# Delta rule and gated layers on one core: the first four chunks solved by rows in two passes, and the whole order written anew

## The chip, the core and the metric

One core of one Trainium2 chip runs the program. TensorE (PE) multiplies, VectorE (DVE), ScalarE (ACT) and GpSimd (POOL) work elementwise, and SyncE (SP) issues most of the transfers. The metric is the device time of one execution in microseconds (us), lower is better.

## The reference

The program computes a delta-rule attention over 768 positions for 4 x 8 heads of width 48, and puts its output through two dense layers with a gate between them.

```python
k_n = k / (np.linalg.norm(k, axis=-1, keepdims=True) + 1e-06)
for t in range(S):                       # S = 768, state is 48 x 48 a head
    y[:, :, t] = np.einsum('bhd,bhde->bhe', q[:, :, t], state)
    v_old = np.einsum('bhde,bhd->bhe', state, kt)
    state = state + bt[:, :, :, None] * np.einsum('bhd,bhe->bhde', kt, vt - v_old)
...
h = x @ w_in                             # x is 3072 x 384, w_in 384 x 2048
g = h - np.tanh(h)
return (g @ w_out).astype(np.float32)    # w_out 2048 x 384
```

## The kernel before

**Chunks and groups.** The 768 positions are cut into 24 chunks of C = 32. In a chunk each of the 32 heads (4 batches x 8) has a 32 x 32 triangular system. Four chunks make a group, so a group has 128 systems, one in each partition, and is solved on DVE. There are six groups; `solve(g, k)` issues step k of group g.

**A group's solve.** PE forms the Gram products of the keys (`gram` for chunks 0 to 3, `pair` for the others, which also forms the query products). `gather` copies four chunks' Gram matrices into one tile, and step 0 transposes it in 32 x 32 blocks so that a partition holds one system. Some eighteen instructions on 32 elements normalize the keys, the square root by Newton steps (for group 0 by ScalarE's table). Then column j of the system is eliminated by two instructions, `times` (a product into the scratch tile `ta`) and `plus`, for j = 1 to 30. In groups 1 to 5 each of them is issued as two instructions over separate columns where 5 < j < 27 (`spans`). A last transposition writes `tt`, the solved triangles, in the layout that PE multiplies with.

**Group 0 is halved.** Its systems are cut into two 16 x 16 triangles that are solved in the same instructions (`JOINED`), j = 1 to 14 only; the missing quarter is put together afterwards for each chunk by two small PE products (`join_a`, `join_b`) with a copy on ScalarE between them (`join_y`) and an addition on DVE (`join_u`).

**Chunk by chunk.** The chunks follow each other through the 48 x 48 states: `keyed` (K, old state times keys and queries), `vsub` (vs), `chunk` (C, solved triangle times values), `spread` (sd, a copy), `answer` (A), the update (U, summed into the PSUM tile `sums`), `keep` (kp, the state copied to SBUF), then the output turned by PE (`turn`, tu) and split into a high and a low part (`x_high` xh, `x_low` xl).

**Dense layers.** Four chunks are a wave of 512 columns; there are six. A wave takes 16 steps f. `hidden` (h) makes 128 hidden features with 9 matmuls, `tanh` (th, ScalarE), `gate` (ga, DVE), `gate_high` and `gate_low` (gh, gl) split the gate's output, and `output` (o) adds 9 matmuls into the PSUM tile `po`. The first wave is done in two halves of 256 columns, z = 0 for chunks 0 and 1, z = 1 for chunks 2 and 3.

**Weights.** The 32 weight pieces of 384 KB are loaded in pairs and split on ScalarE and DVE into two f32r parts: `sign` (dr), `low_bits` (db), `merge` (dm), `high` (dh), `low` (dl). A pair costs ScalarE three and DVE two instructions of 768 elements.

**Order.** The string `ORDER` is the program: each item names an engine and an operation, and an engine executes its items in that order. A wait comes only from data and from buffers that are used again. A load is marked S1 to S4: it is not issued before the load that stands that many loads ahead of it has landed. SP executes its items in order too, so a load that waits for its buffer holds up all loads behind it. `fi:n` issues n matmuls whose result nobody uses.

Of the kernel before, what the change touches and what calls it, by code (L numbers as in the profile page):

```python
# [44 lines left out]
def kernel(ctx: ExitStack, tc: tile.TileContext, kp, kn, vn, beta, w_in, w_out, const, out):  # L45
# [38 lines left out]
    def open_():  # L84
        nc.vector.memset(wz, 0.0)
        nc.vector.memset(sums[32:64, :, :DM], 0.0)

    def const_():
        nc.scalar.dma_start(cs[:, :260], const)
        nc.scalar.activation(wz[:, 0:1], wz[:, 0:1], AF.Sqrt)  # L90
# [34 lines left out]
    def gram(s, slot):  # L125
        ps = hc(bank(slot, f"g{s}"))
        for u in range(16):
            products(s, ps[:, :, :C], live[f"k{s}"], 0, u)
# [37 lines left out]
    nm, ss, zz, sq, gm = small.values()  # L166
    solves = {}

    def solve(g, k, *slots):
        if g not in solves:  # L170
            solves[g] = steps(g)
        solves[g][k](*slots)

    def steps(g):
        halves = g in JOINED
        gs = live[f"gs{g}"]
        V = nc.vector
        ax = lambda: live[f"a{g}"]
        sq3 = lambda: ax()[:, :C * C].rearrange("p (i c) -> p i c", c=C)
        flat = lambda: ax()[:, :C * C]  # L180

        def turn(slot):
            make("sol", slot, f"a{g}", [128, 1056])
            V.transpose(flat(), gs[:, :C * C])

        do = [turn, lambda: V.tensor_copy(sq, flat()[:, ::C + 1])]
        do.append(lambda: V.tensor_scalar(ss, sq, 1e-30, None, ALU.max))
        if g == 0:
# [7 lines left out]
                lambda: V.scalar_tensor_tensor(gm, gm, 4.0, live["bt0"], ALU.mult, ALU.mult),  # L196
                lambda: V.tensor_scalar(nm, nm, 0.5, None, ALU.mult)]
        else:
            do.append(lambda: V.tensor_scalar(nm.bitcast(I32), ss.bitcast(I32), -0.5, 1597463007.0, ALU.mult, ALU.add))
            for _ in range(3):  # L200
                do += [
                    lambda: V.scalar_tensor_tensor(zz, ss, -0.5, nm, ALU.mult, ALU.mult),
                    lambda: V.tensor_tensor(zz, zz, nm, ALU.mult),
                    lambda: V.scalar_tensor_tensor(nm, zz, 1.5, nm, ALU.add, ALU.mult)]
            do += [
                lambda: V.tensor_tensor(nm, nm, sq, ALU.mult),
                lambda: V.tensor_scalar(nm, nm, 1e-6, None, ALU.add),
                lambda: V.tensor_tensor(gm, nm, nm, ALU.mult),
                lambda: V.reciprocal(gm, gm),
                lambda: V.tensor_tensor(gm, gm, live[f"bt{g}"], ALU.mult)]  # L210
        do.append(lambda slot: V.transpose(make("nt", slot, f"nt{g}", [128, C]), nm))
        size = C // 2 if halves else C
        nb = C // size

        def part():
            if halves:
                return ax().rearrange("p (x r) -> p x r", x=2)[:, :, :512].rearrange("p x (i c) -> p x i c", c=C)[:, :, :, :size]
            return sq3()

        P = lambda i, j: part()[:, :, i, j] if nb == 2 else part()[:, i, j]  # L220

        def scale(x):
            block = part()[:, x] if nb == 2 else part()
            V.scalar_tensor_tensor(block, block, -1.0, gm[:, size * x:size * x + size, None].broadcast_to([128, size, size]), ALU.mult, ALU.mult)

        do += [lambda x=x: scale(x) for x in range(nb)]
        do.append(lambda: nc.gpsimd.memset(flat()[:, ::C + 1], 1.0))

        def scratch(j):
            n = size - 1 - j  # L230
            tv = ta[:, j % 2 * 256:j % 2 * 256 + nb * n * j]
            if nb == 2:
                return tv.rearrange("p (x i c) -> p x i c", c=j, x=2), [128, 2, n, j]
            return tv.rearrange("p (i c) -> p i c", c=j), [128, n, j]

        def spans(j):
            if nb == 2 or not 5 < j < 27:
                return (slice(0, j),)
            x = 4 if j < 14 else 10
            return (slice(0, x), slice(x, j))  # L240

        def times(j):
            tv, dims = scratch(j)
            for x in spans(j):
                d = dims[:-1] + [x.stop - x.start]
                V.tensor_tensor(tv[..., x], P(slice(j + 1, size), slice(j, j + 1)).broadcast_to(d),  # L246
                                P(slice(j, j + 1), x).broadcast_to(d), ALU.mult)

        def plus(j):
            tv, _ = scratch(j)  # L250
            for x in spans(j):
                rest = P(slice(j + 1, size), x)
# [582 lines left out]
```

## Time and profile before

| | |
|---|---|
| median of 3 runs | 594.34 us (592.3 to 596.8) |
| span of the profiled execution, first to last instruction | 588.6 us |
| PE busy | 558.4 us, 95% |
| DVE busy | 379.7 us, 65% |
| ACT busy | 187.5 us, 32% |
| granted TensorE clock, mean | 0.985 of full speed |

The page gives the profiled execution's span alone; the median of the runs lies 5.7 us above it, the lowest run 3.7 us. The busy shares are means over a beginning in which PE has little to do and a long rest in which it has no pause, so the stretches are read one by one.

### The profile page before, as it was taken

Reading aid. Unit: us, or ns where it says so; the run is one execution under the profiler, and the core shown is the slowest. Engines: PE = TensorE matmul, PEld = TensorE weight load, DVE = VectorE, ACT = ScalarE, POOL = GpSimd, SP = SyncE. Lnnn points to the kernel's source line nnn. Section 1 sums busy time; section 2 is a strip of 40 time slices with the busy share of each in tenths; the row PEclk is TensorE's granted clock in tenths of the full one; section 3 lists DMA queues with packets and bytes.
Section 4 is the critical chain, followed back from the end, with each engine's and each line's share of the span. In section 5 each row is a group of like instructions: output and inputs, shape, how many; then the busy total and the mean of one; then the engine's idle time right before and its main releaser. Section 6 shows DMA issues by size and latency. Waiting matters only on the chain.

```text
span 588.6 us, 25934 instructions
## 1 busy us (share of the span) xinstructions
PE 558.4 (95%) x11943; PEld 458.4 (78%) x11943; DVE 379.7 (65%) x1089; ACT 187.5 (32%) x330; POOL 39.0 (7%) x44
## 2 busy tenths in 40 slices
PE   4848899999999999999999999999999999999997
PEld 3444788899998888788888788787888888888885
DVE  4899997899768995569965333599824322533242
ACT  1447776333313222232222223132320323322211
POOL 0000001100100000000000000200010000001111
PEclk9967999999999999999999999999999999999999
DMA  7778753331325100433312103221210100000001
GB/s 203 236 235 288 220 157 106 107 96 52 105 94 158 47 14 11 144 86 106 91 48 83 30 1 111 70 63 60 62 29 33 52 2 3 1 33 22 2 0 53
DMA packets 21517, 48.82 MB, mean 83 GB/s; under 512 B 3232, under 2 KB 9760, under 8 KB 21408
## 3 DMA queue, kind: packets, MB, share of 16 engines
q1 hardware_dynamic: 20864, 46.44, 26.0%
q8 instruction: 93, 1.52, 1.1%
q10 hardware_dynamic: 544, 0.72, 0.4%
q14 instruction: 16, 0.13, 0.1%
HBM read 42.44 MB, written 4.72 MB: 80 GB/s over the span
## 4 chain that ended last, share of the span: by engine, by line
PE 87%; DVE 9%; issue 2%; DMA 1%; ACT 1%
PE po L514 35%; PE ph L479 34%; PE sums L361 3%; PE g L123 3%; PE pu L351 3%; PE kk L340 3%; PE py L367 2%; PE py L355 2%; DVE ta L246 2%; DVE a L253 2%; PE px L412 1%; DVE raw L447 1%; DMA k<-in_kp 1%; DVE w L457 1%; DMA raw<-in_w_in 1%
## 5 line engine op out<-in xcount | busy, mean ns | idle before, releaser
L514 PE MATMUL po<-gh,w 128*128 128x512 f32 (+1 forms) x1008 | 221.6, 366 | 0.0
L479 PE MATMUL ph<-xt,w 128*128 128x512 f32 (+1 forms) x1008 | 218.4, 364 | 0.5 <-DVE t L492 0.4
L479 PEld LDWEIGHTS ph<-xt,w 128*128 128x128 f32 x1008 | 170.1, 189 | 31.6 <-DVE t L492 0.5
L514 PEld LDWEIGHTS po<-gh,w 128*128 128x128 f32 x1008 | 168.5, 189 | 30.3 <-DVE gh L502 0.2
L492 DVE TENSOR_TENSOR t<-ph,t 128x512 f32<-128x512 f32 (+1 forms) x112 | 68.2, 611 | 108.6 <-ACT t L487 108.4
L487 ACT ACTIVATE t<-ph 128x512 f32<-128x512 f32 (+1 forms) x112 | 59.7, 538 | 192.7 <-PE ph L479 144.7
L502 DVE TENSOR_TENSOR gh<-t,gh 128x512 fp32r<-128x512 f32 (+1 forms) x89 | 54.4, 614 | 26.0 <-ACT gh L497 25.3
L497 ACT CAST gh<-t 128x512 fp32r<-128x512 f32 (+1 forms) x63 | 35.8, 570 | 83.1 <-PE po L514 52.9
L253 DVE TENSOR_TENSOR a<-a,ta 128x108 f32<-128x108 f32 (+28 forms) x269 | 60.4, 257 | 1.5
L246 DVE TENSOR_TENSOR ta<-a 128x108 f32<-128x108 f32 (+28 forms) x269 | 59.6, 254 | 1.3
L502 POOL TENSOR_TENSOR gh<-t,gh 128x512 fp32r<-128x512 f32 (+1 forms) x23 | 27.4, 1193 | 416.9 <-DVE gh L497 215.0
L351 PEld LDWEIGHTS pu<-v,tt 32*32 32x32 f32 x1536 | 27.8, 106 | 9.5 <-issue 4.1
L351 PE MATMUL pu<-v,tt 32*32 32x48 f32 x1536 | 31.6, 212 | 2.4 <-issue 1.4
L340 PEld LDWEIGHTS kk<-st,k 48*32 48x32 f32 x1472 | 27.8, 105 | 6.8 <-issue 3.8
L367 PE MATMUL py<-ub,pc 32*32 32x48 f32 x1536 | 30.9, 209 | 0.4 <-ACT ub L399 0.3
L355 PE MATMUL py<-st,k 48*32 48x48 f32 x1472 | 31.1, 212 | 0.0
L340 PE MATMUL kk<-st,k 48*32 48x48 f32 x1472 | 30.9, 211 | 0.0
L497 DVE CAST gh<-t 128x512 fp32r<-128x512 f32 (+1 forms) x49 | 18.4, 376 | 18.2 <-PE po L514 17.8
L367 PEld LDWEIGHTS py<-ub,pc 32*32 32x32 f32 x1536 | 26.7, 103 | 1.4 <-ACT ub L399 0.6
L355 PEld LDWEIGHTS py<-st,k 48*32 48x32 f32 x1472 | 27.2, 105 | 0.4 <-DVE t L492 0.4
L361 PEld LDWEIGHTS sums<-ub,kt 32*48 32x48 f32 x1472 | 18.9, 119 | 8.4 <-issue 4.7
L361 PE MATMUL sums<-ub,kt 32*48 32x48 f32 x1472 | 21.9, 205 | 1.8 <-ACT ub L399 1.0
(87 smaller groups left out, 386.7 us busy)
## 6 DMA issues: line engine op xcount, KB each, us to landing
c<-in_kp SPq DMA_DIRECT2D x20, 448.0 KB, 4.6
k<-in_kp SPq DMA_DIRECT2D x20, 448.0 KB, 4.0
raw<-in_w_in SPq DMA_DIRECT2D x16, 384.0 KB, 4.1
raw<-in_w_out SPq DMA_DIRECT2D x16, 384.0 KB, 4.2
v<-in_vn SPq DMA_DIRECT2D x24, 192.0 KB, 2.6
kt<-in_kn SPq DMA_DIRECT2D x24, 192.0 KB, 2.9
out<-o SPq DMA_DIRECT2D x17, 256.0 KB, 3.0
k<-in_kp SPq DMA_DIRECT2D x6, 224.0 KB, 4.5
```

The source lines that it names most:

```text
L246: V.tensor_tensor(tv[..., x], P(slice(j + 1, size), slice(j, j + 1)).broadcast_to(d), P(slice(j, j + 1), x).broadcast_to(d), ALU.mult)
L253: V.tensor_tensor(rest, rest, tv[..., x], ALU.add)
L340: nc.tensor.matmul(hv(live[f"kk{s}"])[q:q + 32, h, :], live[f"k{s}"][rows, 0, 2 * h + b // 2, :], states[s % 2][rows, b // 2, h], start=(h ...
L351: nc.tensor.matmul(hv(live[f"pu{s}"])[rows, h, :], tt[rows, 8 * r + h, :], live[f"v{s}"][rows, h, :], start=True, stop=True)
L355: nc.tensor.matmul(hv(live[f"py{s}"])[q:q + 32, h, :], live[f"k{s}"][rows, 1, 2 * h + b // 2, :], states[s % 2][rows, b // 2, h], start=(h ...
L361: nc.tensor.matmul(sums[HALF[b % 2], b // 2, h * D:h * D + D], live[f"kt{s}"][rows, h, :], live[f"ub{s}"][rows, h], start=(s == 0 and h == ...
L367: nc.tensor.matmul(hv(live[f"py{s}"])[to:to + 32, h, :], live[f"pc{s}"][rows, h, :], live[f"ub{s}"][rows, h, :], start=(s == 0 and h == 0) ...
L479: nc.tensor.matmul(p, wi[:, a, c, :], xt[:, b, c, part], start=(i == 0), stop=(i == len(steps_) - 1))
L487: nc.scalar.activation(t, live[name("ph", w, f, z)][:, :n], AF.Tanh)
L492: nc.vector.tensor_tensor(t, live[name("ph", w, f, z)][:, :n], t, ALU.subtract)
L502: (nc.vector if eng == "V" else nc.gpsimd).tensor_tensor(gh[:, 1, :n], live[name("t", w, f, z)][:, :n], gh[:, 0, :n].bitcast(F32), ALU.sub ...
L514: nc.tensor.matmul(live[f"po{NC * w + c}"][:, part], wo[:, a, 128 * c:128 * c + 128], gh[:, b, :n], start=(f == 0 and (a, b) == SPLIT[0] a ...
```

## The change

Chunks 0 to 3 are no longer halved and joined. Their 128 systems are solved in two passes, chunks 0 and 1 first (x = 0), then chunks 2 and 3 (x = 1). A pass has 64 systems, and each takes two partitions ("lanes"), which hold the even and the odd rows of the inverse. The inverse is built from the identity by rows, from j = 31 down to 1, again with a `times` and a `plus` for each j, on (16 - j//2) x j elements. `times` is now a scalar_tensor_tensor with a per-partition factor. The Gram products of the four chunks go into the PSUM tile `sums` (two strips of 32 columns side by side in the same two banks), and step 0 transposes straight from PSUM, each element written twice. The joins, the four gathers of group 0 and its masks are gone; POOL writes the identity (`ti`).

In groups 1 to 5 `spans` is gone: every `times` and `plus` is one instruction. The fill matmuls use zeros throughout. The whole `ORDER` is another one, with steps of the two passes and of group 1 interleaved, other places for loads and other marks S1 to S4.

```diff
-    def gram(s, slot):
-        ps = hc(bank(slot, f"g{s}"))
-        for u in range(16):
-            products(s, ps[:, :, :C], live[f"k{s}"], 0, u)
+    grams = lambda x: sums.rearrange("p r (h c) -> p (r h) c", h=H)[:, :, C * x:C * x + C]
+
+    def gram(s):
+        for r in range(2):
+            for u in range(16):
+                products(s + r, grams(s // 2)[:, H * r:H * r + H], live[f"k{s + r}"], 0, u)
...
+    def rows(x):
+        ss, zz, sq = (small[n] for n in ("ss", "zz", "sq"))
+        nm, gm = small["nm"], half["gn" if x else "gm"]
+        rate, scratch = cs[:, 160 + C * x:160 + C * x + C], (ta, tb)[x]
...
+        def turn(slot):
+            make("sol", slot, f"as{x}", [128, 1024])
+            V.transpose(full().rearrange("p (i z u) -> p i z u", z=2, u=2 * H),
+                        grams(x).rearrange("p u i -> p i u")[:, :, None].broadcast_to([128, C, 2, 2 * H]))
...
+        def times(j):
+            k, n = j // 2, C // 2 - j // 2
+            to = scratch[:, j % 2 * 136:j % 2 * 136 + n * j].rearrange("p (k c) -> p k c", c=j)
+            V.scalar_tensor_tensor(to, t[:, k:, j:j + 1].broadcast_to([128, n, j]), gm[:, j:j + 1],
+                                   a()[:, j:j + 1, :j].broadcast_to([128, n, j]), ALU.mult, ALU.mult)
+
+        def plus(j):
+            k, n = j // 2, C // 2 - j // 2
+            V.tensor_tensor(t[:, k:, :j], t[:, k:, :j], scratch[:, j % 2 * 136:j % 2 * 136 + n * j].rearrange("p (k c) -> p k c", c=j), ALU.add)
+
+        for j in range(C - 1, 0, -1):
+            do += [lambda j=j: times(j), lambda j=j: plus(j)]
+        do.append(lambda: V.scalar_tensor_tensor(t, t, -1.0, gm[:, None, :].broadcast_to([128, C // 2, C]), ALU.mult, ALU.mult))
+
+        def out_(slot=None):
+            if x == 0:
+                make("sol", slot, "tt0", [128, 1024])
+            to = live["tt0"][:, :32 * C].rearrange("p (u k z) -> p k z u", k=C // 2, z=2)[:, :, :, 16 * x:16 * x + 16]
+            V.transpose(to, t.rearrange("p k (z u) -> p k z u", z=2))
...
-        def spans(j):
-            if nb == 2 or not 5 < j < 27:
-                return (slice(0, j),)
-            x = 4 if j < 14 else 10
-            return (slice(0, x), slice(x, j))
...
 ORDER = """
-V:open A:ka:3:0 S3:lk:2:1 S3:lk:0:2 A:const A:ka:1:3 P:gm:3:0 P:gm:2:1 S2:lb:0:0 P:gm:0:2 S2:lc:4:0 V:gr:0:V:0
...
+V:open A:ka:0:0 S4:lk:1:1 S2:lk:2:2 S3:lv:0:0:0 S3:lk:3:3 P:fi:2:-1 P:fi:2:-1 P:fi:4:-1 P:gm:0 P:fi:3:-1 P:gm:2 A:const
+G:ti V:sv:0:0:0 V:sv:0:1 V:sv:0:2 A:sv:0:3 V:sv:0:4 V:sv:0:5 V:sv:0:6 V:sv:0:7 V:sv:0:8 V:sv:0:9 V:sv:0:12 V:sv:0:13
...
+V:sv:0:31 V:sv:0:86 V:sv:0:32 V:pr:0:V V:sv:0:33 V:sv:0:87 V:sv:0:34 V:sv:0:88 V:sv:0:35 V:sv:0:89 V:sv:0:36 V:mk:5:0
...
+A:mv:2:6 P:A:0:0 P:U:0 P:fi:8:-1 S3:lw:24:10 S2:lv:2:0:0 S3:lw:15:0 S4:lc:9:0 S2:lw:17:0 S3:lw:26:11 V:sv:0:123 V:sv:1:12
...
+A:db:3:A A:mv:3:7 A:dh:4:A:12 A:y:0:A:0 A:kp:0:A P:tu:0:1 A:xh:0:A A:dr:3 A:dr:7 V:dm:5 V:sv:1:28 V:sv:0:141 V:sv:1:29
...
```

In the new order the steps of `sv:0` are numbered 0 to 75 for the first pass (75 writes its half of `tt`) and 76 to 158 for the second.

## Rows read from the trace of the kernel before

**Rows 1.** The page: span, DVE's busy tenths in 40 slices, transfer rate by slice.
```profile
span 588.6 us, 25934 instructions
...
DVE  4899997899768995569965333599824322533242
...
GB/s 203 236 235 288 220 157 106 107 96 52 105 94 158 47 14 11 144 86 106 91 48 83 30 1 111 70 63 60 62 29 33 52 2 3 1 33 22 2 0 53
```
**Rows 2.** Stretches: us, busy of PE, PEld, DVE, ACT, POOL, clock, DMA share, GB/s.
```profile
15.00:20.00 5.00, 2.75 (x39) 1.18 (x39) 2.87 (x13) 0.07 (x1) 0.15 (x1) 1.00 0.55 180
...
40.00:52.00 12.00, 8.67 (x265) 5.28 (x265) 11.69 (x48) 7.92 (x13) 0.15 (x1) 0.50 0.84 270
...
66.40:80.00 13.60, 13.10 (x335) 12.23 (x334) 13.10 (x49) 9.29 (x17) 0.00 (x0) 1.00 0.64 197
...
178.00:259.00 81.00, 81.00 (x1822) 65.07 (x1810) 60.09 (x184) 21.95 (x39) 2.71 (x3) 1.00 0.23 69
```
**Rows 3.** Chain of waits at the start: start, us, what.
```profile
0.80 4.22 DMA k<-in_kp
```
**Rows 4.** Timeline, the solve's start to the first hidden features: start, us, engine, line.
```profile
5.07 2.72 PE L123 MATMUL g<-k 48*32 48x32 f32 x192 [5.07 <-DMA k<-in_kp]
...
11.17 1.25 DVE L184 STREAM_TRANSPOSE a<-gs 128x1024 f32<-128x1024 f32 x1
...
18.13 0.42 DVE L161 TENSOR_TENSOR pc<-g,cs 128x256 f32<-128x256 f32 x1 [1.93 <-PE g L123]
...
66.56 0.56 DVE L426 TENSOR_TENSOR xt<-px,xt 128x384 fp32r<-128x384 f32 x1
```
**Rows 5.** Timeline of PE: work that the new order has earlier or not at all.
```profile
77.99 1.48 PE L123 MATMUL g<-c 48*32 48x64 f32 x128
...
53.14 0.93 PE L361 MATMUL sums<-ub,kt 32*48 32x48 f32 x64 [0.95 <-ACT ub L399]
...
40.84 1.05 PE L323 MATMUL jb<-yj,tn 16*32 16x16 f32 x64 [1.73 <-DVE a L224]
```
**Rows 6.** Groups by line and form: busy us, mean ns of one | idle before.
```profile
L246 DVE TENSOR_TENSOR ta<-a 128x28 f32<-128x28 f32 x2 | 0.4, 190 | 0.0
L253 DVE TENSOR_TENSOR a<-a,ta 128x108 f32<-128x108 f32 x22 | 5.9, 267 | 0.2
L224 DVE SCALAR_TENSOR_TENSOR a<-a,gm 128x1024 f32<-128x1024 f32 x5 | 6.1, 1222 | 0.0
L202 DVE SCALAR_TENSOR_TENSOR zz<-ss,nm 128x32 f32<-128x32 f32 x15 | 2.9, 192 | 0.5
L276 DVE STREAM_TRANSPOSE tt<-a 128x512 f32<-128x512 f32 x1 | 1.1, 1080 | 0.0
...
L442 ACT ACTIVATE raw<-raw,cs 128x768 int32<-128x768 uint8 x15 | 14.8, 1010 | 0.0
L402 ACT COPY st<-sums 112x768 f32<-112x768 f32 x19 | 15.2, 798 | 13.6 <-PE sums L361 13.5
```
**Rows 7.** Timeline of DVE: starts of instructions that do and don't depend on each other.
```profile
20.17 0.25 DVE L246 TENSOR_TENSOR ta<-a 128x88 f32<-128x88 f32 x1
20.46 0.25 DVE L253 TENSOR_TENSOR a<-a,ta 128x88 f32<-128x88 f32 x1
...
23.89 0.95 DVE L447 SCALAR_TENSOR_TENSOR raw<-raw 128x768 int32<-128x768 int32 x1
24.76 0.26 DVE L246 TENSOR_TENSOR ta<-a 128x100 f32<-128x100 f32 x1
```
**Rows 8.** Timeline of DVE in the first wave: residual of chunk 3, subtraction of chunk 4.
```profile
108.43 0.56 DVE L426 TENSOR_TENSOR xt<-px,xt 128x384 fp32r<-128x384 f32 x1
...
109.24 0.55 DVE L345 TENSOR_TENSOR v<-v,kk 128x384 f32<-128x384 f32 x1
```
**Rows 9.** Timeline of PE: fill matmuls at either clock, x11 at full, x7 at half.
```profile
22.53 2.55 PE L556 MATMUL po<-cs 128*128 128x512 bf16 x11
...
49.10 3.09 PE L556 MATMUL po<-cs 128*128 128x512 bf16 x7
```

More of the change, by code (lines that the diff above doesn't have):

```diff
@@ L195, in steps @@
                 lambda: V.reciprocal(gm, gm),
-                lambda: V.scalar_tensor_tensor(gm, gm, 4.0, live["bt0"], ALU.mult, ALU.mult),
+                lambda: V.scalar_tensor_tensor(gm, gm, -4.0, rate, ALU.mult, ALU.mult),
                 lambda: V.tensor_scalar(nm, nm, 0.5, None, ALU.mult)]
         else:
[L199 to L204, printed above, removed]
@@ L220, in steps @@
[L220 to L226, printed above, removed]
+            do += newton(nm, ss, zz, sq, gm) + [lambda: V.scalar_tensor_tensor(gm, gm, -1.0, rate, ALU.mult, ALU.mult)]
+        do.append(lambda: V.transpose(turned[x], nm))
@@ new lines, in rows, with newton @@
+        do.append(out_)
+        return do
+    def newton(nm, ss, zz, sq, gm):
+        V = nc.vector
+        do = [lambda: V.tensor_scalar(nm.bitcast(I32), ss.bitcast(I32), -0.5, 1597463007.0, ALU.mult, ALU.add)]
+        for _ in range(3):
+            do += [
+                lambda: V.scalar_tensor_tensor(zz, ss, -0.5, nm, ALU.mult, ALU.mult),
+                lambda: V.tensor_tensor(zz, zz, nm, ALU.mult),
+                lambda: V.scalar_tensor_tensor(nm, zz, 1.5, nm, ALU.add, ALU.mult)]
+        return do + [
+            lambda: V.tensor_tensor(nm, nm, sq, ALU.mult),
+            lambda: V.tensor_scalar(nm, nm, 1e-6, None, ALU.add),
+            lambda: V.tensor_tensor(gm, nm, nm, ALU.mult),
+            lambda: V.reciprocal(gm, gm)]
@@ L242, in times @@
+            return ta[:, j % 2 * 240:j % 2 * 240 + n * j].rearrange("p (i c) -> p i c", c=j), [128, n, j]
         def times(j):
             tv, dims = scratch(j)
[L244 to L247, printed above, removed]
+            V.tensor_tensor(tv, sq3()[:, j + 1:, j:j + 1].broadcast_to(dims), sq3()[:, j:j + 1, :j].broadcast_to(dims), ALU.mult)
@@ L263, in steps @@
[L263 to L282 removed]
+        do.append(lambda: V.tensor_tensor(sq3(), sq3(), gm[:, None, :].broadcast_to([128, C, C]), ALU.mult))
@@ L313, in join_y @@
-    def join_y(s, slot):
-        nc.scalar.activation(make("yj", slot, f"yj{s}", [128, H, C // 2]), jh(live[f"ja{s}"]), AF.Copy, scale=-1.0)
-    def join_b(s, slot):
-        gs, tn, tt, x = parts(s)
-        pz = jh(bank(slot, f"jb{s}"))
-        for h in range(H):
-            for b in range(4):
-                k, m = slice(32 * b, 32 * b + 16), slice(32 * b, 32 * b + 32)
-                lhs = tn[k, x + h:x + h + 2, :].rearrange("p u j -> p (u j)")
-                nc.tensor.matmul(pz[m, h, :], lhs, live[f"yj{s}"][k, h, :], start=True, stop=True)
@@ L569 @@
         "lc": score_keys, "ld": state_keys, "lv": values, "lb": rates, "lw": weights,
-        "gm": gram, "lt": late, "sp": pair, "gr": gather, "mv": move, "mk": mask, "sv": solve, "tr": triangle,
-        "th0": tanh_table, "ja": join_a, "jy": join_y, "jb": join_b, "ju": join_u, "pr": prep, "K": keyed, "vs": vsub,
+        "ti": identity, "gm": gram, "lt": late, "sp": pair, "gr": gather, "mv": move, "mk": mask, "sv": solve, "tr": triangle,
+        "th0": tanh_table, "pr": prep, "K": keyed, "vs": vsub,
         "C": chunk, "Q": query, "U": lambda s: together((update_product, s)), "A": answer, "sd": spread, "kp": keep, "y": y_copy, "tu": turn, "xh": x_high, "xl": x_low,
```

506 lines of the change are left out of this document (229 added, 277 removed).

## The prediction

> **What bounds the kernel now.** I read the page first. PE's 95% hides two halves: DVE's tenths stand at 8 or 9 from the second slice to the seventh, some 15 to 100 us, with one slice of 7 after it and then 9s again, and fall to 2 to 6 in the second half of the run [rows 1]. So I asked for the stretches. From 178 to 259 us PE is busy all the time, 81.00 of 81.00, and DVE 60.09; from 40 to 52 us it is DVE that is full, 11.69 of 12, with PE at 8.67, part of it matmuls that nobody needs, and at half the clock [rows 2]. The kernel is therefore bound by DVE until the first wave runs, and by PE's list of work behind it. The time is the moment at which the first hidden features can be made, plus PE's list from there, plus what PE still waits.
>
> The timeline gives that moment. The first h group needs chunks 0 and 1, whose last instruction is the residual `xl:1`. It starts at 66.56 and ends at 67.12 us [rows 4]. DVE's own list up to it begins with the transposition at 11.17 us, so it takes 55.95 us, of which two are a stall at the start (a mask at 18.13 us that waited for PE) [rows 4]. Behind 67.12 lie 588.6 - 67.1 = 521.5 us [rows 1].
>
> **When the new list begins.** Keys issued at 0.8 us land after 4.22 us [rows 3], so `gm:0` starts at 5.07 as the first products did; there 192 records took 2.72 us, 0.91 per 64 [rows 4]. `gm:0` is now 128 records and ends near 6.9. Three fills at half clock follow: 0.44 each [rows 9], to 8.2. `gm:2` is again 128 records, but its second half needs chunk 3's keys, marked S3 and thus issued when chunk 1's have landed, at about 5.0; after another 4.22 us they are there at 9.2. With both terms `gm:2` ends between 10.0 and 10.6. Does the transposition of the first pass wait for it? The two grams are separate strips of the same banks, and `gm:2` stands ahead of the transposition in the order. No row shows whether such a read waits, so I keep both ends: 6.9 without the wait, 10.6 with it. I take the later one, 10.4, since nothing in the trace shows two strips of a bank told apart.
>
> **DVE's list to `xl:1`.** Prices first. A two-operand instruction of n elements takes 0.16 us + 1.04 ns x n: 28 elements 190 ns, 108 elements 267, and a scalar_tensor_tensor of 1024 1222 [rows 6]. An instruction that needs the one before it starts 0.04 after its end (20.17 to 20.46 with 0.25 of duration); one that doesn't starts 0.085 before its end (23.89 to 24.76 with 0.95) [rows 7]. So an independent instruction occupies DVE for its duration less 0.085, and a dependent neighbour costs 0.12 more.
>
> Ahead of `xl:1` the new order has 210 DVE instructions:
> - 118 of the two passes' 124 steps. A pass has 62 steps and sum of (16 - j//2) x j = 2856 elements for each of `times` and `plus`; the 118 have some 11,240. 118 x 0.075 + 11,240 x 1.04 ns = 20.5 us.
> - Two transpositions of 1024, the end scaling of 512 and the transposition out of 512. The strided one of 512 took 1080 ns [rows 6], the dense one of 1024 1.25 us [rows 4]: 2 x 1.17 + 0.6 + 1.0 = 3.9. Read from PSUM with a stride and twice, the first kind is not in the trace; it is bounded by 1.25 and twice 1080 ns. In the strided rows it is the writing that is strided; here the writing is dense, so I take 1.25. The other end adds 1.8.
> - 45 instructions on 32 elements, 192 ns [rows 6] less 0.085, four reciprocals among them longer: 5.4.
> - Group 1's transposition, scaling and 20 unsplit steps: 1.2 + 1.1 + 4.2 = 6.5.
> - Nine weight instructions at 0.95 - 0.085: 7.8. Seven masks of 0.42 [rows 4], three scalings, one subtraction and one residual of 0.55: 4.7.
>
> That is 48.8. Of the 209 neighbours 33 depend on each other: 33 x 0.12 = 4.0. ScalarE's square root 0.3, the residual itself 0.56: 53.7 us. From 10.4 it ends at 64.1, against 67.12: **3.0 us earlier**. The joins that go are off this sum in PE and ScalarE; on DVE they were four additions and the half solve, and the interleaved lanes cost more than that. What is won is the start: no gathers, no masks, no stall at 18 us.
>
> `times` has a per-partition factor, which no row shows. Below, nothing changes (the scalar_tensor_tensor rows lie on the two-operand line); above, twice the slope as in the strided transposition, 57 x 92 x 1.04 ns = 5.5 us. I take nothing, it is the same instruction, and keep 5.5 for the range.
>
> **What hides the rest.** PE's own work ahead of the first h is 29 us of dense work in 64, and the chunk chain has room: chunk 0's triangle leaves DVE at about 42 us, and the first instruction on DVE that needs chunk 0's state, `vs:1`, comes at 10.4 + 44.8 = 55.2. If that cover goes, each us is a us at the end (second rival). POOL's identity is written before the transposition. The unsplit steps of groups 2 to 5 fall where DVE has 21 us idle of 81 [rows 2]: nothing.
>
> **PE's list behind the first h.** Only three real packs and three fills have left it, the rest is the same by count: `sp:8` 1.48, `U:1` 0.93, `jb:3` 1.05 [rows 5], the fills 0.5: **4.0 us less**. In the new order `sp:8` and `U:1` are done while PE waits for `xl:1`.
>
> **What PE waits after it.** From 66.4 to 80 us PE is busy 13.10 of 13.60 [rows 2], so little was lost there. DVE's list from `xl:1` to `xl:3` is now 71 instructions, 32.1 us by the same prices, where it took 41.9 (67.12 to 108.99) [rows 4, 8], because some of group 1's steps now come later. To chunk 4's subtraction the two are level: 10.4 + 98.9 = 109.3 against 109.79 [rows 8], but by then PE has five more groups of 256 columns behind it. DVE feeds PE no later than before, and I leave PE's waits as they were.
>
> **Sum.** 588.6 - 3.0 - 4.0 = 581.6 us of span. The profiled span lies 5.7 under the median of the runs; with that, 587.3 us, 1.2% faster.
>
> **The rivals.**
> 1. *The transposition doesn't wait for the second gram.* The list begins at 6.9, 3.5 us sooner: 583.8. DVE's lead on `xl:3` may save 3 us of PE's waits too: 580.5. For it: separate columns. Against: `gm:2` writes the same banks ahead of it. 0.2.
> 2. *The fetch becomes the bound, and the change is slower.* On ScalarE the copy of chunk 0's state, `kp:0`, stands behind `db:3`, which needs weight piece 7. Up to that piece the new order loads 10.6 MB. The rates by slice (203, 236, 235, 288 GB/s of 14.7 us each) [rows 1] give 9.9 MB by 44.1 us and 10.6 by 46.7. Behind it 1.01 for `db:3`, three shorter ones, 0.80 for `kp:0` [rows 6] and K:1: `vs:1` is free at some 52, 3 us ahead of DVE. Beyond 50 us every us of landing counts, beyond 57 the change is slower than 594.3. At the lowest rate of the loading stretch, 180 GB/s [rows 2], it lands at 59: 596.3. For it: SP now waits with `lv:2` for chunk 0's update, and ScalarE's items are in a row behind loads. Against: the mean before was 236. 0.1.
> 3. *Given back, no change.* PE does less ahead of the first h. The granted clock was at half from 40 to 52 us, when PE was busy 8.67 of 12 [rows 2], and fills of 512 columns then cost 0.44 instead of 0.23 [rows 9]. If the first eight groups of 256 columns run at that level, they take 8 x 1.07 longer, less 3.3 us that PE waits there for DVE anyway: 5 more, 592.6. The same place is reached by the dearer transpositions and `times` (7.3 us). For it: new idle time of PE. Against: eight fills and `sp:8` stand right ahead of the first h. 0.2. [...]
> 4. *Interleaving hides nothing*, so that a step of one lane waits for the other's: 176 neighbours x 0.12 = 21 us, 608. [Rows 7] speak against it. 0.03. [...]
>
> The forecast itself has the rest, 0.47, and its own range is 583 to 592.
>
> **How the numbers follow.** A measurement of this kernel tells about 1% from no change. Faster by over 1% is below 588.4: rival 1 and three quarters of the forecast, 0.55. Slower by over 1% is above 600.3: rival 4, a third of rival 2 and unforeseen waits of a new order, 0.10. The rest, 0.35, is within 1%. The range reaches from rival 1 at 580.5 to rival 2 at 596.3 and so to 597.
>
> **What would show it.** Right: the first transposition near 10.4 us, `times` on the 0.16 + 1.04 ns line and starting before its neighbour's end, `xl:1` ending near 64, DVE without gaps before it, PE without new idle from 64 to 115 us. Wrong: idle on DVE before `vs:1` with ScalarE or a load as releaser (rival 2), half clock behind 64 us (rival 3), the transposition at 7 us (rival 1), or new waits of PE late in the run, where I have looked for none beyond counting.

## The result, and the profile after

The changed kernel takes 600.15 us (median of 13 runs, 597.22 to 604.91) against 593.59 of the kernel before beside it: ratio 1.0115, interval 1.0089 to 1.0142, 1.2% slower. Forecast were 587.3 us and a range up to 597.0, so the time lies outside the range and on the other side. The profiled execution is the longest of the 13, 604.9 us for a span of 603.2; run e10 below holds a second one with a span of 596.6, and where sizes matter both are given.

The page of the changed kernel, the lines that answer to [rows 1]:

```profile
span 603.2 us, 24778 instructions
...
PE 558.4 (93%) x11425; PEld 457.1 (76%) x11425; DVE 404.3 (67%) x1001; ACT 181.5 (30%) x324; POOL 23.6 (4%) x30
...
DVE  1999999989776886749875545597964333443434
...
PEclk8667799999998999999999999989999999999999
...
GB/s 224 264 267 140 220 67 197 164 82 53 17 91 52 167 64 28 122 58 61 142 29 114 26 19 45 59 95 29 76 30 111 1 3 2 2 52 1 0 2 53
```

Stretches of the changed kernel, with the columns of [rows 2] (us, busy of PE, PEld, DVE, ACT, POOL, clock, DMA share, GB/s):

```profile
40.00:52.00 12.00, 7.18 (x255) 4.66 (x256) 11.89 (x49) 4.79 (x9) 0.00 (x0) 0.67 0.36 120
...
66.00:71.00 5.00, 5.00 (x148) 3.05 (x141) 5.00 (x16) 3.83 (x6) 0.00 (x0) 0.76 0.59 168
...
177.90:180.80 2.90, 0.35 (x40) 0.22 (x33) 0.34 (x1) 0.00 (x0) 0.00 (x0) 1.00 0.03 6
181.10:184.40 3.30, 3.30 (x25) 3.18 (x21) 0.00 (x0) 0.86 (x2) 0.00 (x0) 0.50 0.02 5
184.50:259.00 74.50, 74.16 (x1544) 59.90 (x1546) 58.36 (x138) 20.28 (x36) 1.43 (x2) 1.00 0.31 90
```

DVE is full from the start of its list, as forecast, and the steady middle is as it was (74.16 of 74.50). New is a stretch such as 177.9 to 180.8, in which almost nothing runs (PE 0.35 us and DVE 0.34 of 2.90), and behind it a stretch at half the clock. [Rows 2] have PE busy in all of 178 to 259.

Two landmarks divide the difference. The first hidden features start at 70.81 us (69.92 in e10) in place of 66.4: 3.5 to 4.4 us later, where the forecast had them 2 us earlier. Behind them, what PE's items took beyond their own dense time (the time that they take back to back) adds up to 23.0 us in the kernel before, 36.7 in the changed one, 30.6 in e10: 7.6 to 13.7 us more. PE's list behind the landmark became shorter, 499.2 us of such dense time before, 495.7 after.

The head first. Timeline of the changed kernel's start, PE and DVE (start, us, engine, line, what, in brackets the idle time before and what ended it):

```profile
4.79 1.86 PE L123 MATMUL sums<-k 48*32 48x32 f32 x128
...
7.51 0.92 PE L123 MATMUL sums<-k 48*32 48x32 f32 x84
10.79 0.86 PE L123 MATMUL sums<-k 48*32 48x32 f32 x44 [2.36 <-issue]
...
11.69 1.25 DVE L194 STREAM_TRANSPOSE as<-sums 128x1024 f32<-128x1024 f32 x1 [10.68 <-PE sums L123]
...
15.43 0.25 DVE L215 SCALAR_TENSOR_TENSOR ta<-tn,gmh,as 128x31 f32<-128x31 f32 x1
15.72 0.19 DVE L220 TENSOR_TENSOR tn<-tn,ta 128x31 f32<-128x31 f32 x1
...
37.55 1.26 POOL L292 TENSOR_SCALAR_AFFINE_SELECT a<-a 128x1024 f32<-128x1024 f32 x1 [30.84 <-DVE sq L260]
37.57 1.28 DVE L260 TENSOR_SCALAR ss<-sq 128x32 f32<-128x32 f32 x1
...
66.74 2.73 PE L518 MATMUL po<-wz 128*128 128x512 bf16 x8
...
68.22 0.55 DVE L392 TENSOR_TENSOR xt<-px,xt 128x384 fp32r<-128x384 f32 x1
...
69.40 1.48 PE L123 MATMUL g<-c 48*32 48x64 f32 x128
```

The reader sees five things. The second Gram product stands still for 2.4 us in its middle, without a cause that the profile knows ("issue"). The transposition waits for its end. `times` (L215) takes 0.25 us on 31 elements where `plus` (L220) takes 0.19. An instruction on 32 elements takes 1.28 us while POOL works, and ends with POOL's. And when the residual of chunk 1 ends at 68.77, PE still has fills at 0.34 us each and `sp:8` ahead of it.

### The profile page after: what moved, and what is told of

The parts are those of the page before. It is cut to its first block, busy times and chain, and to the rows that moved or that the text cites. A ratio compares the mean times of both kernels' runs of the same rounds, so it can differ in the third digit from the quotient of the medians.

```text
span 603.2 us, 24778 instructions
## 1 busy us (share of the span) xinstructions
PE 558.4 (93%) x11425; PEld 457.1 (76%) x11425; DVE 404.3 (67%) x1001; ACT 181.5 (30%) x324; POOL 23.6 (4%) x30
## 4 chain that ended last, share of the span: by engine, by line
PE 77%; DVE 17%; issue 2%; ACT 2%; DMA 1%; DVEq 0%
PE po L480 31%; PE ph L445 31%; PE sums L327 3%; PE pu L317 3%; PE kk L306 2%; PE py L333 2%; PE py L321 2%; DVE tn L220 2%; PE g L123 2%; DVE tt L285 2%; PE px L378 1%; DVE ta L215 1%; DVE tb L215 1%; DVE raw L413 1%; DVE ta L273 1%
## 5 line engine op out<-in xcount | busy, mean ns | idle before, releaser
L480 PEld LDWEIGHTS po<-gh,w 128*128 128x128 f32 x1008 | 171.5, 191 | 31.3 <-DVE w L423 0.7
L468 DVE TENSOR_TENSOR gh<-t,gh 128x512 fp32r<-128x512 f32 (+1 forms) x101 | 60.6, 602 | 15.1 <-ACT gh L463 13.6
L277 DVE TENSOR_TENSOR a<-a,ta 128x30 f32<-128x30 f32 (+9 forms) x150 | 50.4, 336 | 3.4
L273 DVE TENSOR_TENSOR ta<-a 128x30 f32<-128x30 f32 (+9 forms) x150 | 49.4, 329 | 3.3
L463 ACT CAST gh<-t 128x512 fp32r<-128x512 f32 (+1 forms) x57 | 30.1, 531 | 59.5 <-PE po L480 31.1
L463 DVE CAST gh<-t 128x512 fp32r<-128x512 f32 (+1 forms) x55 | 22.2, 405 | 30.0 <-PE po L480 28.8
L306 PE MATMUL kk<-st,k 48*32 48x48 f32 x1472 | 32.3, 212 | 1.2 <-issue 0.9
L468 POOL TENSOR_TENSOR gh<-t,gh 128x512 fp32r<-128x512 f32 x11 | 14.8, 1345 | 290.4 <-DVE gh L463 180.1
L123 PE MATMUL g<-c 48*32 48x64 f32 x1280 | 16.4, 234 | 9.9 <-DMA c<-in_kp 7.1
L123 PEld LDWEIGHTS g<-c 48*32 48x32 f32 x1280 | 14.1, 109 | 13.4 <-issue 10.0
```

Source lines behind the costliest of these rows:

```text
L273: V.tensor_tensor(tv, sq3()[:, j + 1:, j:j + 1].broadcast_to(dims), sq3()[:, j:j + 1, :j].broadcast_to(dims), ALU.mult)
L277: V.tensor_tensor(sq3()[:, j + 1:, :j], sq3()[:, j + 1:, :j], tv, ALU.add)
L306: nc.tensor.matmul(hv(live[f"kk{s}"])[q:q + 32, h, :], live[f"k{s}"][rows, 0, 2 * h + b // 2, :], states[s % 2][rows, b // 2, h], start=(h ...
L463: (nc.scalar.copy if eng == "A" else nc.vector.tensor_copy)(gh[:, 0, :n], live[name("t", w, f, z)][:, :n])
L468: (nc.vector if eng == "V" else nc.gpsimd).tensor_tensor(gh[:, 1, :n], live[name("t", w, f, z)][:, :n], gh[:, 0, :n].bitcast(F32), ALU.sub ...
L480: nc.tensor.matmul(live[f"po{NC * w + c}"][:, part], wo[:, a, 128 * c:128 * c + 128], gh[:, b, :n], start=(f == 0 and (a, b) == SPLIT[0] a ...
```

## The experiments

In the table and the sums of stalls, a PE wait is put down to a block start where it lies at the instruction named below; sums are over waits above 0.35 us behind the first hidden features. A wait is counted from the moment at which PE would have gone on at its dense pace, which gives some 0.2 us more than the idle time that a line of the profile has in brackets. All ratios are against the kernel before, run beside each kernel.

### Does PE get its instructions in time?

The "issue" waits have a pattern. I numbered PE's instructions (weight loads, matmuls, semaphore instructions) in the order of each trace. Here are the waits above 0.5 us behind the first hidden features, and the one inside the second Gram product:

```
kernel     wait at, length    instruction   modulo 256
before     86.80  1.43        4544          192
before     92.03  1.02        4800          192
before    112.08  0.99        6081          193
before    334.54  0.58       17088          192
changed     8.24  2.55         448          192
changed   142.97  1.12        6593          193
changed   155.33  1.50        7360          192
changed   164.05  1.40        7872          192
changed   177.96  2.75        8641          193
changed   517.54  1.26       22208          192
```

The instruction queue carries 16 KB transfers, 89 of them. The DMA view of the changed kernel from 141.5 to 143.0 us has nothing else:

```profile
DMA packets 1, 0.02 MB, mean 11 GB/s; under 512 B 0, under 2 KB 0, under 8 KB 0
...
q8 instruction: 1, 0.02, 4.5%
```

It starts at 141.72, takes 1.08, and PE goes on at 144.09, 1.3 us after the landing; the others end 1.3 to 1.6 us after theirs (the one in the second Gram product at 10.79, its transfer landed at 9.40). The counts agree: 11,425 matmuls and as many weight loads are 89.3 times 256, beside 89 transfers; in the kernel before 11,943 of each are 93.3 times 256, and its queue carried 93. So PE gets its instructions in blocks of 256, and at these ten places it waited for one. The kernel's description above says that a wait comes only from data and from buffers that are used again, and leaves this one out. So theory R: a block that PE runs through faster than the next one comes makes it wait, and a pack of 128 small matmuls with their loads is a block in 1.2 to 1.3 us (those that begin at 154.02 and 514.01 us in the changed kernel). Shifting the list by some instructions that do nothing must then move the waits, and shifting it by 256 must not.

**e3, e9: the kernel before, shifted ahead of the first wave by 140 and by 256.** `ad:n` is n matmuls of 32 x 32.

```diff
-P:fi:5:-1 P:h:0:1:0:0
+P:fi:3:-1 P:ad:72:-1 P:h:0:1:0:0      (e3; e9: P:ad:130:-1)
```

> The kernel before, with two of the five fill matmuls right ahead of the first hidden features taken out and 72 tiny matmuls put in: its list is shifted by 140 instructions from there on, the work is the same. R: as it stands, the kernel before has only four such stalls behind the first wave's start (4.0 us in its trace); shifted, the sum gives 15 us. 8 to 13 us slower, ratio 1.013 to 1.022. D: the tiny matmuls cost under 1 us where PE waits anyway; ratio 0.998 to 1.002.

Measured: 1.0364 (1.0283 to 1.0446), 612.45 us. Twelve stalls, 18.2 us in sum, in place of four with 4.0; 13.7 us at half clock behind the first hidden features where there was none.

> As e3, with 130 tiny matmuls in place of 72: the list of the kernel before is shifted by 256 instructions, one whole block. Theory R: the same blocks begin at the same items again, so the 20 us of e3 go, and what stays is the tiny matmuls' own time, at most 2 us: ratio 0.999 to 1.005, stalls behind 66 us as before the shift (4.0). Rival T (the tiny matmuls themselves, or a clock that falls behind them, cost the 20 us of e3): nearly twice as many cost more, ratio 1.04 or above.

Measured: 1.012 (1.0061 to 1.018). Six stalls, 5.4 us. 14 of the 20 us are gone, but not all: the tiny matmuls stand where PE was about to start the first wave, which now begins at 70.34 in place of 66.36 us, and the clock is at half from 69.4 to 79.6 us. So both were run again with the tiny matmuls in a pause.

**e13, e14: the same shifts in PE's pause at 29.5 us.**

```diff
-P:fi:10:-1 P:ja:1:2
+P:fi:10:-1 P:ad:70:-1 P:ja:1:2        (e13; e14: P:ad:128:-1)
```

> The kernel before with 70 tiny matmuls in PE's pause at 29.5 us, where it waits 1.9 us: shift by 140 instructions, nothing added near the first wave. Theory R (refills): as e3, stalls of 15 us or more in sum behind 66 us in place of 4.0, 12 to 22 us slower, ratio 1.02 to 1.037. Rival T (the tiny matmuls ahead of the first wave and the clock behind them made e3 slow): ratio under 1.006.

> The same with 128 tiny matmuls, 256 instructions, one whole block. R: the blocks begin where they did in the kernel before; stalls behind 66 us 3 to 6 us in sum, no half clock there, ratio 0.998 to 1.004. T: as e13 or slower.

Measured: e13 1.0358 (1.0292 to 1.0425), 613.85 us; e14 1.0028 (0.9987 to 1.0069), 594.0 us. The chain of waits from 66 to 300 us, its "issue" pieces (start, us), first e13, then e14:

```profile
67.67 3.09 issue
...
87.45 1.48 issue
...
101.00 1.56 issue
...
105.46 1.48 issue
...
122.19 1.54 issue
...
160.56 1.10 issue
...
175.07 1.85 issue
...
189.80 1.79 issue
...
253.08 2.02 issue
```

```profile
69.32 1.28 issue
...
94.55 1.34 issue
...
176.13 2.21 issue
```

And PE in one long stretch of each, e13 first:

```profile
75.00:500.00 425.00, 409.76 (x9315) 344.12 (x9314) 286.85 (x851) 126.78 (x232) 25.85 (x26) 0.99 0.24 70
```

```profile
75.00:500.00 425.00, 420.60 (x9563) 353.23 (x9562) 289.97 (x859) 132.00 (x241) 26.57 (x26) 1.00 0.24 70
```

In both traces the first hidden features come later than in the kernel before (73.67 us in e13, 74.29 in e14, for 66.36), so the head is not what divides the two. From there to the end e13 takes 537.8 us, with 13 stalls of 17.6 us in sum; e14 takes 522.5 us, with 3 of 4.6, and the kernel before 522.2. What the later head costs e14 in the median can't be read from this one trace: the execution took 598.5 us, where the median is that of the kernel before.

With 256 idle instructions more, a whole block, the kernel is as fast as before; with 140 it is 20 us slower. So the time of the kernel before depends by 3.6% on where its blocks begin. Its own order stands well to them; the changed order has its packs at other block starts.

**e1, e2, e8: the changed kernel shifted** by 38 and 172 instructions, and with the early turn (below) by 40: `P:lt:1:2 P:ad:19:-1`, `P:ad:86:-1`, `P:ad:20:-1`, in a pause at 18 us.

> The changed kernel with 19 tiny matmuls (32 x 32, result unused) more, in a pause of PE at 18 to 25 us. Theory R, code refills: PE stalls where its instructions run out. In the traces of both kernels the long PE waits without a data reason (1.1 us at 143, 1.6 at 155, 1.4 at 164, 2.7 at 178 us of the changed kernel) all lie at instruction 192 + 256 n of PE's list, counting loads, matmuls and semaphore instructions, and each ends some 1.4 us after a 16 KB transfer of instructions has landed. 19 matmuls are 38 instructions: the blocks then begin elsewhere in the list, and the four waits go; two others (1 us at 126, 1.3 us at 505) come. A sum over blocks that PE runs through in under 2.9 us gives 2.4 us of such stalls in place of 5.3. So 3 to 6 us faster than the changed kernel: 594 to 597 us, ratio to the kernel before 1.000 to 1.007, and no wait over 1 us at the four items. Rival D, data: the waits come from late results of the new order; they stay at the same items with the same length, 600 us, ratio 1.009 to 1.014.

Measured: 1.015 (1.0097 to 1.0204), no gain. The waits of 143, 155 and 178 us left their items as R said, but others came that the sum had not foreseen (1.1 at 71, 1.3 at 87, 1.8 at 132, 2.3 at 512 us): 7.7 us in place of 8.9.

> The same with 86 tiny matmuls in the same pause: 172 instructions. R: by the same sum this is the worst place for the blocks, 11.4 us of stalls in place of 5.3, among them 1.0 to 1.7 us each at about 158, 170, 231, 282, 318, 368 and 504 us; 3 to 7 us slower than the changed kernel, 603 to 607, ratio 1.016 to 1.023. D: as before the shift, ratio 1.009 to 1.014, waits at the same four items.

Measured: 1.0526 (1.0476 to 1.0576), 622.9 us, some 23 us slower than the changed kernel where 3 to 7 were expected. Fourteen stalls, 23.5 us, up to 3.3 each, and five stretches at half clock, 17.1 us. Against the changed kernel's trace (8.9 us, 6.8 at half clock) that is 14.6 of stalls, half of 10.3, 5.2, of clock, and 2.5 from a later landmark: 22 us, for 20.1 between the two spans.

> Early turn with 20 tiny matmuls in PE's pause at 20 us, 40 instructions. The sum over blocks is made anew from the traces of all runs so far: the next block's transfer starts some 1 to 1.4 us after PE has begun a block, takes 1.0, and PE goes on 1.4 us after it landed, so a block run through in less than some 3.5 us stalls. By it e4 has 9.3 us of stalls (6.4 in its trace) and this 4.6, with the worst shift 18.8. R: 2 to 5 us faster than e4, ratio 0.994 to 0.999. Against: the shift by 38 of the unmoved kernel took only 1.2 us of stalls away and no time; then ratio 1.000 to 1.005.

Measured: 1.009 (1.0044 to 1.0136), 597.9 us, no gain, and 4 us above e4's 593.56; stalls 8.0 us. The profiled execution, 593.91 us, is one of the shortest of its ten, so it doesn't show what the median lost. R stands, but my sum over blocks finds the bad places and not the good ones: when a transfer starts differs by some us from block to block and run to run (4.05 us behind PE's entry into a block at 174 in the changed kernel, mostly 0.8 to 1.3), and I can't say why.

**e10: the changed kernel again.**

> The changed kernel itself once more, for a second profiled execution: the one at hand took 604.91 us, the longest of its 13 runs. R: stalls at the same block starts (the items at 143, 155, 164, 178 and 517 us), their lengths differing by up to 1 us with the transfers; behind 66 us 6 to 10 us in all. If the stalls are at other items each time, they are no matter of the order. Ratio 1.009 to 1.014.

Measured: 1.0102 (1.004 to 1.0163). Stalls at the same starts (142.2, 154.9, 160.1, 164.1, 510.9), 6.6 us; the 2.75 us at 178 did not come again, nor the half clock behind it:

```profile
70.00:596.00 526.00, 511.35 (x9954) 426.94 (x9954) 346.68 (x783) 152.97 (x283) 20.43 (x19) 1.00 0.21 63
```

The places belong to the order, the lengths to the run.

### What set the first hidden features?

**e4: the transposition ahead of the second Gram product.**

```diff
-P:gm:0 P:fi:3:-1 P:gm:2 A:const
-G:ti V:sv:0:0:0 V:sv:0:1
+P:gm:0 V:sv:0:0:0 P:fi:3:-1 P:gm:2 A:const
+G:ti V:sv:0:1
```

> The changed kernel with the first pass's transposition ahead of the second Gram product in the order. If it waited only for its place behind that product, it now starts at about 6.7 us in place of 11.69, and the first pass's whole list on DVE begins 4.8 us sooner. Theory H (the head counts, DVE bounds it): the residual of chunk 1 ends at about 64 in place of 68.8 and the whole is 3 to 5 us faster than the changed kernel, ratio 1.003 to 1.007. Rival F (the fetch bounds it): DVE waits for weights, for keys of group 1 or for chunk 0's state, the residual comes less than 2 us sooner, ratio 1.008 to 1.014. If the second product must now wait for the transposition to have read, it starts at 8.0 us, which costs nothing before the second pass.

Measured: 1.002 (0.9979 to 1.0061), 593.56 us, 6.6 us under the changed kernel's 600.15 (5.0 under the 598.56 of e10): the whole loss, within the noise.

```profile
6.26 1.25 DVE L194 STREAM_TRANSPOSE as<-sums 128x1024 f32<-128x1024 f32 x1 [5.25 <-PE sums L123]
...
7.56 0.92 PE L123 MATMUL sums<-k 48*32 48x32 f32 x84 [0.59 <-DVE as L194]
```

The transposition starts 5.4 us sooner, the residual ends at 63.39 (68.77), the first hidden features start at 65.25 (70.81). DVE had no new idle time: the fetch does not bound (rival F and the second rival of the prediction fall). The product now waits for the transposition in turn, so the program's waits don't tell the two strips apart, and the order alone decides who waits. The stalls at block starts stayed what they were in e10 (6.4 us for 6.6), so the gain is the head's.

**e7: `times` without the per-partition factor.**

```diff
+            if j == C - 1:
+                V.tensor_tensor(a(), a(), gm[:, :, None].broadcast_to([128, C, C]), ALU.mult)
-            V.scalar_tensor_tensor(to, t[:, k:, j:j + 1]..., gm[:, j:j + 1], a()[:, j:j + 1, :j]..., ALU.mult, ALU.mult)
+            V.tensor_tensor(to, t[:, k:, j:j + 1]..., a()[:, j:j + 1, :j]..., ALU.mult)
```

> Early turn with times of the two passes as a plain two-operand product; the rows of the Gram matrix are scaled once a pass by one instruction on 1024 elements. In the changed kernel's trace times takes 0.25 us on 31 elements and plus 0.19: theory P, the per-partition factor costs 0.053 us each, so times falls to 0.19 on 31 and 0.29 on 126 elements, 3.3 us in all; the scalings cost 1.13 each: the residual of chunk 1 about 1 us earlier. PE's own list sets the first hidden features, so the time stays within 1 us of e4, ratio 0.999 to 1.003. Rival: the interleaved strided reading makes times dear, not the factor; then it stays at 0.25, the residual is 2 us later, ratio 1.002 to 1.006.

Measured: 1.0018 (0.9981 to 1.0055). Groups by line and form in the first 75 us, changed kernel first, then e7 (count | busy us, mean ns | idle before):

```profile
L215 DVE SCALAR_TENSOR_TENSOR ta<-tn,gmh,as 128x126 f32<-128x126 f32 x3 | 1.0, 349 | 0.0
...
L220 DVE TENSOR_TENSOR tn<-tn,ta 128x126 f32<-128x126 f32 x3 | 0.9, 285 | 0.0
...
L215 DVE SCALAR_TENSOR_TENSOR ta<-tn,gmh,as 128x30 f32<-128x30 f32 x2 | 0.5, 250 | 0.0
```

```profile
L217 DVE TENSOR_TENSOR ta<-tn,as 128x126 f32<-128x126 f32 x3 | 0.9, 287 | 0.0
...
L217 DVE TENSOR_TENSOR ta<-tn,as 128x30 f32<-128x30 f32 x2 | 0.4, 184 | 0.0
```

The factor costs some 0.06 us an instruction at 30 as at 126 elements, the strides nothing (287 ns on 126, where `plus` takes 285). From the transposition's start to the residual's e7 needs 55.6 us, e4 56.6. The first hidden features come 1.0 us sooner (64.20 for 65.25), but the time shows nothing of it; the profiled execution has a stall of 2.2 us at 238 with half clock behind it, where e4 has 0.6 and full clock.

**e5, e15: PE's fills ahead of it.** e5 takes the eight fills behind `tu:1` away, adds sixteen in earlier pauses and 114 tiny matmuls, to a shift of 256; e15 replaces them in e12 (below) by tiny ones: `P:tu:1:2 P:ad:8:-1`.

> Early turn (run e4, 593.56 us) with the fill matmuls moved: 8 more behind chunk 1's K, 8 between its C and A, where PE stands idle for 1.7 and 2.2 us, and none of the 8 behind tu:1 that ran at half the clock from 61.3 to 63.9; 114 tiny matmuls at 18 us make the shift of the list 256 instructions, so that the blocks behind it begin where they did. Theory C (the clock ahead of the first hidden features costs): at full clock A:1, U:1, tu:1 and sp:8 take 3.4 us in place of 6.0 and the fills 2.6 go, so the first hidden features come with the residual of chunk 1 at 62.9 in place of 65.25, and the whole is 2 to 3 us faster than e4: 591, ratio 0.996 to 0.999. Rival (PE only waits later): the first h groups are followed by waits for DVE, under 1 us faster than e4, ratio 1.000 to 1.004.

Measured: 1.0047 (1.0004 to 1.0089). Inside the edited stretch the blocks did move: PE stalls 3.2 us at 51 and 2.6 at 64.3, in `sp:8`, and the first hidden features come at 67.95. It says nothing of the clock.

> e12 with the eight fill matmuls ahead of sp:8 (1.9 us at half clock) replaced by eight tiny ones, so that the blocks stay. Theory C (PE's list sets the first hidden features): they come at 62 in place of 63.5 and the whole is 1 to 1.5 us faster than e12, 591, ratio 0.995 to 0.999. Rival: U:1, tu:1 and sp:8 then follow each other so fast that the block they fill stalls, or the clock stays at half in the first hidden groups; no gain, ratio 0.998 to 1.003.

Measured: 1.0029 (0.9989 to 1.007), no gain; the first hidden features start at 64.2, e12's at 63.53. `sp:8` in e15, timeline of PE:

```profile
59.71 0.30 PE L123 MATMUL g<-c 48*32 48x64 f32 x4
61.65 0.43 PE L123 MATMUL g<-c 48*32 48x64 f32 x25 [1.64 <-DVE xt L402]
62.70 1.57 PE L123 MATMUL g<-c 48*32 48x64 f32 x99 [0.62 <-issue]
```

It needs a PSUM bank that DVE's residual of chunk 0 still reads, and then the next block. So the fills mostly covered a wait that DVE sets. What the half clock ahead of the landmark costs by itself stays open.

### DVE's part

**e6: the split of `times` and `plus` back in groups 1 to 5** (`spans` as before, on e4).

> Early turn with the split of times and plus back in groups 1 to 5, as the kernel before has it. In the changed kernel's trace an unsplit step starts 0.03 us after its neighbour's end where nothing stands between them, some 0.1 us more a column than split, 2 us a group. Theory D (late DVE makes PE wait behind the first wave's start, at C:4, K:18 and o:3:6): 2 to 4 us faster than e4, ratio 0.995 to 0.999, and the 1.95 us at K:18 shrink. The prediction's claim (the unsplit steps cost nothing): ratio 1.000 to 1.004, as e4.

Measured: 1.0006 (0.997 to 1.0043), as e4; the wait in K:18 is 1.86 (1.95 in the changed kernel). The prediction's claim holds, the unsplit steps cost nothing that can be measured.

**e11: chunk 16's residual ahead of five steps of group 5**, on e4: `V:sv:5:23` to `V:sv:5:27` moved behind `V:xl:16`. The place, in the changed kernel:

```profile
390.79 1.30 POOL L468 TENSOR_TENSOR gh<-t,gh 128x512 fp32r<-128x512 f32 x1 [110.30 <-ACT gh L463]
392.04 1.26 POOL L292 TENSOR_SCALAR_AFFINE_SELECT a<-a 128x1024 f32<-128x1024 f32 x1
```

```profile
390.69 0.42 DVE L161 TENSOR_TENSOR pc<-g,cs 128x256 f32<-128x256 f32 x1
391.03 1.10 DVE L240 SCALAR_TENSOR_TENSOR zz<-ss,nm 128x32 f32<-128x32 f32 x1
392.17 1.17 DVE L241 TENSOR_TENSOR zz<-zz,nm 128x32 f32<-128x32 f32 x1
393.36 0.19 DVE L242 SCALAR_TENSOR_TENSOR nm<-zz,nm 128x32 f32<-128x32 f32 x1
```

```profile
401.06 0.20 PE L321 MATMUL py<-st,k 48*32 48x48 f32 x1 [1.60 <-DVE xt L392]
```

> Early turn (e4) with chunk 16's x_high and x_low ahead of five steps of group 5 on DVE. In the traces of the changed kernel and of e4 PE waits 1.8 to 1.95 us inside K:18 for this residual, and DVE is late there by two instructions of 32 elements that took 1.10 and 1.16 us in place of 0.19, each ending with an instruction on POOL. Theory D: the residual comes 1.2 to 1.4 us sooner, PE waits 0.7 or less, the whole is 1 to 1.5 us faster than e4, ratio 0.998 to 1.001. Rival: the wait moves to the next DVE result (the subtraction of chunk 18), no gain, ratio 1.002.

Measured: 1.0009 (0.9974 to 1.0044), 593.32 us: not to be told from e4. The wait in K:18 did shrink, to some 0.6 us here and 0.68 in e12, which has the same edit. But PE now waits 0.8 and 0.7 us in C:18, where e4 has no such wait: as the rival said, in part.

**e12: all of it** (e4, e6, e7, e11, and the masks of chunks 6 and 7 where POOL's select runs).

> What helped or cost nothing, together: early turn, split steps (e6), plain times (e7), chunk 16's residual earlier, and two masks that read PSUM placed where POOL's select runs, so that 0.7 us of DVE's wait for POOL is used. Theory: head about 1 us, K:18 1.3 us, on e4: 591, ratio 0.996 to 1.000. If only the refills and the clock behind them decide, it is within 1 us of e4: ratio 1.000 to 1.004.

Measured: 0.9992 (0.9963 to 1.0022), 592.31 us, the first hidden features at 63.53, stalls 7.7 us. They start 1.7 us sooner than in e4, but PE then waits 1.6 us inside the first groups, up to 66.46, for a mask on DVE (0.3 us in e4). The best version found, level with the kernel before, not better.

## Why the prediction was wrong

**Right.** DVE bounds the kernel up to the first wave and PE's list behind it; the transposition waits for the second gram; the interleaved lanes do overlap (`times` and `plus` of the other lane start 0.08 us before the neighbour's end, so rival 4 falls); the fetch stays hidden, the unsplit steps cost nothing; PE's list behind the first hidden features became 3.5 us shorter (3.1 in e10; 4.0 forecast).

**Term 1, the start: 10.4, measured 11.69 (11.14 in e10).** The step that failed is the cause of the wait in the second gram. I held it to wait for chunk 3's keys; it waited for PE's instructions, 2.4 us: 84 of its 128 products had run by then, 20 of them with chunk 3's keys. Without this stall it would have ended at about 9.3, so that 10.4 came as near as it did is luck. And the term counted as given what the order could change: placed ahead, the transposition starts at 6.26 (e4).

**Term 2, DVE's list: 53.7 us, measured 57.1.** The step "I take nothing" for `times`' factor was mis-sized: 59 of them took 18.3 us where the line of 0.16 us + 1.04 ns x n gives 15.3, 3.0 us more (in e7, without the factor, 59 took 14.7: it is the factor). My upper bound of 5.5 held it. 1.1 us more came from POOL's select, for which the sum had no term, and the dependent neighbours were 0.9 us cheaper. With the start: the residual at 68.77 in place of 64.1.

**Cover.** "In the new order `sp:8` and `U:1` are done while PE waits for `xl:1`" failed by 2 us: with fills at half clock, `U:1` and `sp:8`, PE's list came to the first hidden features after the residual (70.81 against 68.77, and 65.25 against 63.39 in e4). `sp:8` stands in that list and can't begin before the residual of chunk 0 has been read out of its bank (e15), so part of these 2 us is DVE's all the same. [Rows 9] had the price of a fill at half clock; I used it for rival 3 and not for this list. Rival 3 saw the half clock, but behind the landmark, not ahead of it.

**Term 4, PE's waits behind it: unchanged, measured 7.6 (e10) to 13.7 us more.** This is the largest step that failed: "DVE feeds PE no later than before, and I leave PE's waits as they were". By the idle time of the profile, behind 66 us (the wait at 155 us, which the profile puts on DVE, lies at a block start and is counted there):

```
PE waits, us                     before   changed   e10
at block starts                  3.1      7.4       5.2
for results of DVE or ScalarE    0.6      5.9       6.4
```

So DVE and ScalarE do feed PE later, 5.3 to 5.8 us of it. K:18's wait for chunk 16's residual is 1.6 to 1.7 of these; the rest are three waits for solved triangles (`tt`, 1.3 to 1.4 together) and single ones of 0.2 to 0.6 us for masks, weights and copies, of which none was taken out by itself. Blocks, of which the prediction knew nothing, add 2.1 to 4.3. In the profiled execution two waits (178 and 399 us) also had 3.4 us each at half clock behind them, which cost 1.7 each. That makes 7.9 us in e10 and 13.0 in the profiled execution. The prediction named "new waits of PE late in the run, where I have looked for none beyond counting" as what would make it wrong, and so it was: I compared counts of instructions, not where the packs stand against each other, and not when each result comes. Both were there to be asked about: the waits without a cause in the kernel before (1.43, 1.02 and 0.99 us), and DVE's load late in the run. I read DVE's tenths as "2 to 6 in the second half", but slices 27 to 29 have 9, 9 and 8; there the kernel before has PE full and DVE busy for 40.46 of 44.10 us (columns of [rows 2]), and there K:18's wait came:

```profile
382.60:426.70 44.10, 44.10 (x1104) 35.61 (x1104) 40.46 (x146) 13.74 (x24) 0.37 (x1) 1.00 0.21 62
```

**The sum** was made against the span of one execution, 588.6 us, a short one. e10 is nearer to the changed kernel's median: 596.6 is 8.0 above 588.6 where 7.0 below was forecast. Of these 15 us the landmark has 5.8 (69.92 for 64.1), the waits 7.6, the list 0.5 to 0.9; some 1 us is left. Two slips in the prediction are small: the slice of 7 is itself the seventh, and rival 1's 583.8 less 3 is 580.8, not 580.5.

## What to carry to other kernels

Ahead of a rewritten order, number the instructions of the engine that bounds and look at what stands in each block of 256: here packs of small matmuls next to each other ran out of instructions (1.12 and 1.50 us at 142.97 and 155.33), and an edit that adds or drops a few instructions moves every block behind it, which was worth up to 20 us. A trial of an order is therefore also a trial of its block starts; shift a kernel by a few idle instructions, in a pause, before a difference of a per cent is put down to the idea. And where one engine starts the critical list, its first item belongs directly behind what it needs: one item's place was worth 6.6 us. Equal counts of work don't make equal waits: ask for each late result, in the stretches where both engines are nearly full, whether the new order still has it in time.

## What the runs showed of the hardware that was not expected

- PE's instructions come in transfers of 16 KB (89 of them in the changed kernel, 93 in the kernel before). The next block's transfer starts mostly 0.8 to 1.3 us after PE has begun a block, takes 0.9 to 1.7, and PE, where it waits for it, goes on 1.3 to 1.6 us after it landed. In the traces of the two kernels, behind 66 us, two of the three blocks that PE ran through in under 2 us were followed by a stall (1.12 and 1.50 us), four of the 24 that took 2 to 3.6 us (0.99 to 1.43), and three of the 130 that took more (0.58, 1.02 and 2.75).
- Behind PE's wait of 2.75 us at 178 the granted clock, 1.00 from 68.4 us until then, fell to 0.50 from 181.1 to 184.4 us; 18 matmuls of 256 columns took 3.71 us there and 2.14 elsewhere. So this wait cost more than its length; e10's wait of 1.85 us at 394 had no half clock behind it.
- While POOL's select or its subtraction ran, a DVE instruction on 32 elements took 1.10 to 1.28 us in place of 0.18 to 0.19 and ended with POOL's, five times in the changed kernel (37.57, 189.38, 271.45, 391.03 and 392.17 us). Two longer ones took longer too: a weight instruction on 768 elements 1.71 us for 0.95 (109.26), a `plus` on 150 elements 1.38, where the `times` ahead of it took 0.31 (431.25). Three that read PSUM beside POOL took their usual time: two masks 0.42 (108.93 and 390.69), a gate on 512 elements 0.69 (540.49).
- A per-partition factor makes a scalar_tensor_tensor 0.06 us longer at 30 as at 126 elements (250 for 184 ns, 349 for 287).
